# Moving the split weights and the gated tiles to other addresses of SBUF in a kernel of window attention and a SwiGLU gate

## The chip, the cores and the metric

The kernel runs on one core of a Trainium2 chip. The metric is the time of one execution on the device in microseconds; 855.66 us is the median of three runs of the kernel before.

## The reference

For 2048 tokens of width 512: a layer norm without scale or shift gives `xn`. Two branches read it. Branch A is attention with 32 heads of width 16, causal, each token seeing itself and the 255 before it, followed by an output projection. Branch B is a SwiGLU feed-forward with 1792 hidden columns. The output is `x + A * silu(B)`, all in float32.

```python
xn = layernorm(x)
q, k, v = split(xn @ wqkv)                    # 32 heads of 16
p = softmax(where(0 <= i - j < 256, q @ k.T / 4, -1e9))
s = (p @ v) @ wo
g = silu((silu(xn @ w_gate) * (xn @ w_up)) @ w_down)
return x + s * g
```

## The kernel before

**Splitting.** Every projection is computed from operands that are split into a high part (rounded to the type float32r) and a low part (what the rounding lost, also float32r). A product takes three matmuls: high by high, high by low and low by high; low by low is dropped (`PAIRS`). So each weight block exists as two tiles, `wh` and `wl`, the normed activations as `xh` and `xl` (together `xn`), the gated hidden values as one tile `hh` with both parts, and the attention output before `wo` as `oh`, which uses the same buffers as `hh`. Weights are split on the chip: a DMA brings a raw block `wr`, ScalarE rounds it into `wh` (line 474), GpSimd subtracts to get `wl` (line 459).

**Tiling.** The tokens are taken in four chunks of 512. The dense work is a list of 120 units, written out in `ORDER`: A (a pair of head groups' q and k), V (values), G (one block of 128 gate and up columns), D (a quarter of the hidden columns through the down projection, one half of the output columns) and W (`wo`). Unit number n of this list uses two pairs of weight buffers, numbers 2n and 2n+1 modulo 6. So a unit whose number leaves rest 0 after division by 3 has the buffers 0 and 1, rest 1 has 2 and 3, rest 2 has 4 and 5. The numbers are n = 2 for G0.0, 3 for G0.1, 113 for G3.13, 114 to 117 for D3.2.0, D3.2.1, D3.3.0 and D3.3.1, 118 and 119 for W3.0 and W3.1.

**Halves of TensorE.** Each contraction of 128 is done as two of 64: rows 0 to 63 of the array work on one item of a unit, rows 64 to 127 on another (line 491 for all dense matmuls, shown as `64*128`). The two halves run side by side, each with its own order, and meet only in the visits that multiply probabilities with values (`pv`, line 1204). Within a half every matmul needs its own weight load, and the load for the next matmul runs while the present one streams.

**Who is stationary and who moves.** In A and G the weights `wh`, `wl` are loaded into the array and 512 columns of `xh` or `xl` stream through. In V, D and W it is the other way round: 128 columns of activations (`xh`, `xl`; `hh`; `oh`) are loaded and 256 columns of weights stream. In the last chunk's W the activations stand in the buffers of `xn`. Attention scores (lines 1013 and 1167) load columns of q or k and stream up to 384 columns of k or q.

**The order of the work** is fixed when the program is built: a planner with estimated costs emits the instructions of all engines in one order, and only semaphores act at run time. The planner knows nothing of addresses.

**Addresses.** One tile pool (`pers`) holds everything in SBUF. A tile gets its place when its tag first appears in the program, one tag behind the other, each rounded up to 32 bytes; a tag that comes again reuses the place. The tiles that matter here and the rest of their byte address in a partition after division by 256, as the program before is laid out:

| tiles | address | modulo 256 |
|---|---|---|
| `q`, `k` | 19,200 to 49,920 | 0 |
| `xh`, `xl` (four tiles of 8192 bytes) | 67,840 to 100,608 | 0 |
| `gp` (the down projection's sums) | 100,608 | 0 |
| `p` (probabilities) | 109,376 | 64 |
| 12 tiles of 2048 bytes that are handed out for passing values | 136,704 on; 183,936 on | 0; 128 |
| `wr`, two tiles | 146,944; 159,296 | 0; 64 |
| `wh`, `wl` number 0 and 1 | 151,040 to 159,232 | 0 |
| `wh`, `wl` number 2 and 3 | 163,392 to 171,584 | 64 |
| `wh`, `wl` number 4 and 5 | 175,680 to 183,872 | 64 |
| `hh` buffer 7 | 171,584 | 64 |
| `hh` buffers 0 to 6 (also `oh`) | 198,272 to 228,736 | 128 |

Slices that one matmul reads start at multiples of 512 bytes inside these tiles, so the rests of the table are those of the operands.

Of the kernel before, what the change touches and what calls it, by code (L numbers as in the profile page):

```python
# [9 lines left out]
F32 = mybir.dt.float32  # L10
F32R = mybir.dt.float32r
# [6 lines left out]
P = 128  # L18
# [9 lines left out]
TC = 512  # L28
# [9 lines left out]
NHID = 8  # L38
# [27 lines left out]
def tile_window_attention_swiglu_gate(  # L66
# [12 lines left out]
    pers = ctx.enter_context(tc.tile_pool(name="pers", bufs=1))  # L79
# [122 lines left out]
    ks = [pers.tile([P, 2, HALO + TC], F32R, name=f"k{i}") for i in range(3)]  # L202
    vt = pers.tile([P, VT, VROW], F32, name="v")
    xn = [[pers.tile([P, KC, TC], F32R, name=f"x{'hl'[s]}{i}") for s in range(2)] for i in range(2)]
    gp = pers.tile([P, 4, D], F32, name="gp")

    def constants():
# [1246 lines left out]
    while True:  # L1454
        now[0] = max(front[0], min(clock))
        while marks and marks[-1][0] <= work[0] / PACE - LEAD:
            _, fn, a = marks.pop()
# [12 lines left out]
        if not any(extra):  # L1470
            s = work[0] / PACE - LEAD
# [67 lines left out]
```

## Time and profile before

| | us |
|---|---|
| median of three runs | 855.66 (853.76 to 855.67) |
| the profiled execution | 856.13 |
| its span, first to last instruction | 854.3 |
| TensorE matmul busy in the span | 847.2 (99%), 11,950 matmuls |
| weight loads | 786.4 (92%) |
| VectorE, ScalarE, GpSimd busy | 485.3, 496.5, 602.1 |
| the 16 DMA engines, mean busy share | 58.8% by the main queue |

In the profile, PE is TensorE, PEld its weight loads, DVE VectorE, ACT ScalarE, POOL GpSimd. A matmul's duration in it is its passage through the array, with its end modelled; matmuls of a half follow each other sooner than that duration. How fast a half works is read from the starts: the distance from the start of one matmul to the start of the next in the same half. The timeline gives starts to 0.01 us, so a run of ten or more matmuls gives that distance to about 1 ns.

### The profile page before, as it was taken

The page shows a single profiled execution, that of the slowest core. Times are in us where ns is not written, and L with a number is a line of the kernel's source. Part 1 is how long each engine was busy: PE and PEld are TensorE (multiplying, and loading weights), DVE is VectorE, ACT ScalarE, POOL GpSimd, SP SyncE. Part 2 cuts the span into 40 slices and gives each one's busy share as a digit, 9 for nine tenths or more (in the row PEclk, how much of TensorE's full clock was granted, in tenths as well). Part 3 has the DMA queues.
Part 4 walks back from the last instruction along what each step waited for, and adds up shares of the span by engine and source line. Part 5 has one row for each costly group of instructions (what it writes and reads, how often), then busy time and mean ns, then how long its engine had stood idle before and what let it go on. Part 6 is the DMA issues. An engine that isn't in the chain of part 4 may idle for free.

```text
span 854.3 us, 29720 instructions
## 1 busy us (share of the span) xinstructions
PE 847.2 (99%) x11950; PEld 786.4 (92%) x11950; DVE 485.3 (57%) x1628; ACT 496.5 (58%) x1055; POOL 602.1 (70%) x637
## 2 busy tenths in 40 slices
PE   9999999999999999999999999999999999999998
PEld 8899988989999999999999999989999989998998
DVE  4265465655566666555566765566665656554333
ACT  4345566555675566545677566565566766556532
POOL 7556566667686876655779784665667897868866
PEclk9999999999999999999999999999999999999999
DMA  4765554477677955355577886355656767724351
GB/s 152 212 190 166 159 151 136 120 191 182 160 186 207 282 148 129 102 134 154 149 198 197 215 211 196 112 142 154 170 122 165 197 191 205 193 84 147 114 157 57
DMA packets 67661, 139.59 MB, mean 163 GB/s; under 512 B 12722, under 2 KB 21426, under 8 KB 67524
## 3 DMA queue, kind: packets, MB, share of 16 engines
q1 hardware_dynamic: 67220, 137.17, 58.8%
q8 instruction: 94, 1.54, 0.8%
q10 hardware_dynamic: 304, 0.52, 0.2%
q14 instruction: 43, 0.35, 0.1%
HBM read 107.74 MB, written 29.62 MB: 161 GB/s over the span
## 4 chain that ended last, share of the span: by engine, by line
PE 96%; DMA 2%; POOL 1%; issue 1%; ACT 0%; DVE 0%; SPq 0%; POOLq 0%; DVEq 0%; ACTq 0%
PE u L491 19%; PE d L491 19%; PE g L491 17%; PE a L491 11%; PE pv L1204 8%; PE vp L491 5%; PE c L1167 5%; PE s L491 5%; PE b L1013 5%; DMA wr<-wdn 1%; DMA xt<-x 1%; PE xp L513 0%; POOL wl L459 0%; POOL rs L273 0%; POOL p L1141 0%
## 5 line engine op out<-in xcount | busy, mean ns | idle before, releaser
L459 POOL TENSOR_TENSOR wl<-wr,wh 128x512 fp32r<-128x512 f32 (+1 forms) x240 | 298.1, 1258 | 140.5 <-ACT wh L474 122.0
L1021 DVE CUSTOM_DVE_ANT_0 jk<-b,maskb 128x384 bf16<-128x384 f32 (+2 forms) x512 | 271.4, 530 | 124.2 <-PE b L1013 66.3
L1128 ACT ACTIVATE p<-c 128x384 f32<-128x384 f32 (+1 forms) x480 | 208.3, 496 | 128.7 <-PE c L1167 116.2
L491 PE MATMUL d<-wh,hh 64*128 64x256 f32 x1792 | 252.4, 279 | 0.0
L491 PEld LDWEIGHTS d<-wh,hh 64*128 64x128 f32 x1792 | 217.4, 185 | 0.4
L491 PE MATMUL d<-wl,hh 64*128 64x256 f32 x896 | 195.9, 279 | 0.0
L474 ACT ACTIVATE wh<-wr 128x512 fp32r<-128x512 f32 (+1 forms) x239 | 142.1, 619 | 62.5 <-PE u L491 15.4
L491 PE MATMUL g<-xh,wl 64*128 64x512 f32 x448 | 173.3, 396 | 0.6 <-issue 0.6
L491 PE MATMUL g<-xl,wh 64*128 64x512 f32 x448 | 173.4, 395 | 0.0
L491 PE MATMUL u<-xh,wl 64*128 64x512 f32 x448 | 173.1, 396 | 0.0
L491 PE MATMUL g<-xh,wh 64*128 64x512 f32 x448 | 172.9, 394 | 0.0
L491 PE MATMUL u<-xl,wh 64*128 64x512 f32 x448 | 172.7, 396 | 0.0
L491 PE MATMUL u<-xh,wh 64*128 64x512 f32 x448 | 171.6, 395 | 0.0
L491 PEld LDWEIGHTS d<-wl,hh 64*128 64x128 f32 x896 | 141.3, 185 | 0.8 <-issue 0.4
L1141 POOL TENSOR_SCALAR_AFFINE_SELECT p<-p 128x512 f32<-128x512 f32 x128 | 81.0, 636 | 73.6 <-ACT p L1128 71.7
L1013 PE MATMUL b<-k,q 48*128 48x384 f32 (+2 forms) x512 | 112.6, 331 | 0.0
L1167 PE MATMUL c<-q,k 49*128 49x384 f32 (+1 forms) x704 | 103.8, 294 | 0.0
L491 PE MATMUL a<-xl,wh 64*128 64x512 f32 (+1 forms) x264 | 93.1, 389 | 0.0
L491 PE MATMUL a<-xh,wl 64*128 64x512 f32 (+1 forms) x264 | 92.7, 389 | 0.1
L491 PE MATMUL a<-xh,wh 64*128 64x512 f32 (+1 forms) x264 | 92.6, 390 | 0.0
L491 PEld LDWEIGHTS u<-xl,wh 64*128 64x128 f32 x448 | 82.5, 185 | 3.8 <-issue 1.0
L491 PEld LDWEIGHTS u<-xh,wh 64*128 64x128 f32 x448 | 82.2, 185 | 3.4 <-DVE ho L488 0.4
(104 smaller groups left out, 2040.3 us busy)
## 6 DMA issues: line engine op xcount, KB each, us to landing
wr<-wgu SPq DMA_DIRECT2D x56, 512.0 KB
k<-qkd SPq DMA_DIRECT2D x48, 192.0 KB
wr<-wqk SPq DMA_DIRECT2D x16, 512.0 KB
qkd<-qkh SPq DMA_DIRECT2D x32, 256.0 KB
qkd<-qkl SPq DMA_DIRECT2D x32, 256.0 KB
q<-qkd SPq DMA_DIRECT2D x64, 128.0 KB
wr<-wdn SPq DMA_DIRECT2D x16, 512.0 KB
od<-ev SPq DMA_DIRECT2D x32, 256.0 KB
```

The costliest lines, as they stand in the source:

```text
L459: nc.gpsimd.tensor_tensor(lo, raw[j][:, n], f32(hi), op=ALU.subtract)
L474: do("S", t, 0.13 + 0.00078 * m, lambda: nc.scalar.activation(hi, raw[j][:, n], AF.Copy), after_high, sl)
L491: return nc.tensor.matmul(pb, a, b, start=first, stop=last, skip_group_check=True)
L1013: nc.tensor.matmul(pb[:, :w], qs[u % 3][r : r + 48, p, qb * P : (qb + 1) * P], ks[u % 3][r : r + 48, p, lo : lo + w], start=True, stop=True,)
L1021: nc.vector.tensor_tensor_reduce(junk[:, :n], pb[:, :n], maskb[:, 3 * P - n :], 1.0, -3.0e38, ALU.add, ALU.max, m[:, col : col + 1],)
L1128: nc.scalar.activation(t[:, h, :], pc[:, a:b], AF.Exp, scale=DH ** -0.5)
L1141: nc.gpsimd.affine_select(s, s, [[0, 4], [1, P]], ALU.is_ge, 0.0, base=0, channel_multiplier=-1)
L1167: nc.tensor.matmul(pc[:, at0 : at0 + w], ks[u % 3][r : r + 49, p, k0 : k0 + P], qs[u % 3][r : r + 49, p, qb * P : qb * P + w], start=(i == ...
L1204: nc.tensor.matmul(pbs[r][0][32 * j : 32 * j + 32, q0:q1], vt[half(r), (4 * c + kb) % VT, VW * (4 * g + j) : VW * (4 * g + j) + 32], t[hal ...
```

## The change

Right behind the four tiles of `xn` the program names the tags of the twelve split weight tiles, then a tile of 64 bytes that nothing uses, then the eight tags of the gated buffers. Nothing is computed with these tiles here; the names only fix where the tags lie. All later tiles, `gp`, `p`, the passing tiles and `wr` among them, move accordingly. No instruction is added, removed or moved.

```diff
     xn = [[pers.tile([P, KC, TC], F32R, name=f"x{'hl'[s]}{i}") for s in range(2)] for i in range(2)]
+    for n in range(6):
+        for s in "hl":
+            pers.tile([P, 512], F32R, name=f"w{s}_{n}", tag=f"w{s}{n}", bufs=1)
+    pers.tile([P, 16], F32, name="gap")
+    for n in range(NHID):
+        pers.tile([P, 2, TC], F32R, name=f"hr_{n}", tag=f"hr{n}", bufs=1)
     gp = pers.tile([P, 4, D], F32, name="gp")
```

## The prediction

> **What bounds the kernel now.** I read the page first, then the chain of work that ended last, then the groups of instructions by shape, and last the timeline of TensorE row by row, since the change acts on addresses alone and no summed view tells one buffer from another.
>
> ```profile
> span 854.3 us, 29720 instructions
> PE 847.2 (99%) x11950; PEld 786.4 (92%) x11950; DVE 485.3 (57%) x1628; ACT 496.5 (58%) x1055; POOL 602.1 (70%) x637
> PEclk9999999999999999999999999999999999999999
> PE 96%; DMA 2%; POOL 1%; issue 1%; ACT 0%; DVE 0%; SPq 0%; POOLq 0%; DVEq 0%; ACTq 0%
> ```
>
> TensorE is busy throughout at the full clock, and 96% of the chain is its own work. Whatever changes the rhythm of the matmuls shows in the time nearly one to one; 4% of the chain is something else and would not shrink. The two halves of the array run side by side, so the time follows the sum of the distances from start to start within one half.
>
> ```profile
> L491 PE MATMUL d<-wh,hh 64*128 64x256 f32 x1792 | 252.4, 279 | 0.0
> L491 PE MATMUL d<-wl,hh 64*128 64x256 f32 x896 | 195.9, 279 | 0.0
> L491 PE MATMUL g<-xl,wh 64*128 64x512 f32 x448 | 173.4, 395 | 0.0
> L491 PE MATMUL a<-xl,wh 64*128 64x512 f32 x248 | 90.9, 396 | 0.0
> L491 PE MATMUL vp<-wh,xh 64*128 64x256 f32 x256 | 59.2, 280 | 0.0
> L491 PE MATMUL s<-wh,oh 64*128 64x256 f32 x384 | 53.1, 280 | 0.0
> L459 POOL TENSOR_TENSOR wl<-wr,wh 128x512 fp32r<-128x512 f32 x224 | 286.7, 1295 | 127.9 <-ACT wh L474 110.5 <-DMA den<-od 6.9 <-PE c L1167 6.7
> ```
>
> There are 6 x 448 + 3 x 248 = 3432 matmuls of 512 columns in G and A, 1716 a half, and 2688 of D, 768 of V, 768 of W with 256 columns. Their durations (279, 395) hide the rhythm, so the starts decide. All the readings below are starts of one half.
>
> **What the rhythm depends on.** G0.0 (n = 2, weights at rest 64) and G0.1 (n = 3, weights at rest 0) ran side by side, one in each half; these are the first and last rows of either.
>
> ```profile
> 27.03 0.40 PE L491 MATMUL u<-xl,wh 64*128 64x512 f32 x1
> ...
> 27.28 0.39 PE L491 MATMUL g<-xh,wh 64*128 64x512 f32 x1
> ...
> 29.79 0.39 PE L491 MATMUL g<-xh,wl 64*128 64x512 f32 x1
> 29.82 0.39 PE L491 MATMUL u<-xl,wh 64*128 64x512 f32 x1
> ```
>
> `u` of G0.0 makes 12 steps in 2.79 us, 232.5 ns each; `g` of G0.1 makes 11 steps in 2.51 us, 228.2 ns each. The shape, the moving operand's rest (0) and the stretch of time are the same; what differs is where the weights lie. A second pair, `u` of G0.1 (10 steps) and, late and undisturbed by attention, `g` and `u` of G3.13 (n = 113, rest 64; 35 steps of one half):
>
> ```profile
> 33.20 0.39 PE L491 MATMUL u<-xl,wh 64*128 64x512 f32 x1
> ...
> 35.51 0.39 PE L491 MATMUL u<-xh,wl 64*128 64x512 f32 x1
> ...
> 809.83 0.39 PE L491 MATMUL g<-xh,wh 64*128 64x512 f32 x1
> ...
> 818.00 0.39 PE L491 MATMUL u<-xh,wl 64*128 64x512 f32 x1
> ```
>
> That is 2.31 us / 10 = 231.0 ns with weights at 0, and 8.17 us / 35 = 233.4 ns with weights at 64. Sorting all steps of 512 columns by the rest of the weights loaded meanwhile, stalls left out, gives 231.5 ns (1,357 steps) and 233.4 ns (1,734 steps), of which these rows are a part. The neighbour half's addresses make no difference in that sorting.
>
> For 256 columns I write (rest of the moving weights, rest of the loaded activations). D3.2.0 is (0, 128) and D3.2.1 is (64, 128); one row of low weights to the same row of the next block is three steps in either half.
>
> ```profile
> 822.15 0.39 PE L491 MATMUL d<-wl,hh 64*128 64x256 f32 x2
> ...
> 824.64 0.37 PE L491 MATMUL d<-wl,hh 64*128 64x256 f32 x2
> ...
> 825.71 0.33 PE L491 MATMUL d<-wl,hh 64*128 64x256 f32 x2
> ...
> 827.75 0.39 PE L491 MATMUL d<-wl,hh 64*128 64x256 f32 x2
> 828.57 0.28 PE L491 MATMUL d<-wl,hh 64*128 64x256 f32 x1
> ...
> 831.39 0.28 PE L491 MATMUL d<-wl,hh 64*128 64x256 f32 x1
> ```
>
> D3.2.0: 2.49 us / 21 = 118.6 ns. D3.2.1: 2.04 us / 18 = 113.3 ns. D3.3.0 in one half, mostly (64, 128) again: 2.82 us / 24 = 117.5 ns. So one placing shows two rhythms, and the better of them only where the rests differ by 64. Over the whole trace (0, 128) averages 118.7 ns (971 steps) and (64, 128) 117.0 (1,472). The last W is (64, 0) with 45 steps, V3.1 (n = 90) is (0, 0) with 14:
>
> ```profile
> 842.43 0.39 PE L491 MATMUL s<-wh,xl 64*128 64x256 f32 x2
> ...
> 847.73 0.39 PE L491 MATMUL s<-wh,xl 64*128 64x256 f32 x2
> ...
> 657.84 0.28 PE L491 MATMUL vp<-wh,xh 64*128 64x256 f32 x1
> ...
> 659.51 0.28 PE L491 MATMUL vp<-wh,xl 64*128 64x256 f32 x1
> ```
>
> (64, 0) takes 5.30 us / 45 = 117.8 ns and (0, 0) takes 1.67 us / 14 = 119.3 ns.
>
> **The change part by part.** *Where things land.* `xn` ends at 100,608, a multiple of 256. Twelve tiles of 2048 bytes end at 125,184, so every `wh` and `wl` has rest 0. 64 bytes later the eight gated buffers of 4096 bytes start at 125,248, rest 64, and end at 158,016. `gp` goes from 0 to 64, `p` from 64 to 128, the passing tiles from 0 and 128 to 64 and 192, `wr` from 0 and 64 to 64 and 128. The instructions, their order, the semaphores and the DMAs' sizes and queues stay.
>
> *G and A.* 1,837 of the 512-column steps, 918 a half, now have weights at 64 loaded under them and get weights at 0. A gain of 233.4 - 231.5 = 1.9 ns each over the whole trace; the quoted stretches bound it by 232.5 - 231.0 = 1.5 and 233.4 - 228.2 = 5.2. 918 steps at 1.5, 1.8 and 5.2 ns make 1.4, 1.65 and 4.8 us; I take -1.65, near the average, since it has all chunks in it.
>
> *D and the first six W.* All become (0, 64), the difference that (64, 128) has now. 496 steps a half come from (0, 128), 830 from (64, 128). If the difference decides, the first gain 118.7 - 117.0 = 1.7 ns and the others nothing: -0.85 us. (0, 64) does occur, where D loads from buffer 7 with weights at 0: 156 scattered steps, 118.0 ns on average, but each between two or three slower (0, 128) ones. At 118.0 the sum is -496 x 0.7 + 830 x 1.0 = +0.5 us. I take -0.6, most of the way to the first, because buffer 7's steps stand in slower company. Upper gain: 5.3 ns (118.6 - 113.3) for 496 steps, -2.6 us.
>
> *V and the last W.* They go from (64, 0) to (0, 0): 484 steps a half at +1.5 ns, +0.7 us by the two stretches.
>
> *Attention scores.* They stream k or q at rest 0, and 149 steps a half of 384 columns load weights from 64 meanwhile, later from 0. At three quarters of 1.8 ns that is -0.2 us; it may be nothing. `pv` streams `p`, whose rest shifts by 64, against value columns that start at every multiple of 4 bytes, so its 2,816 matmuls meet all differences before and after: nothing.
>
> *The other engines.* Their operands keep shape and type. GpSimd's subtraction has 127.9 us of idle time in front of its 224 pieces, and by its operands' rests its pieces average 1291 to 1307 ns; 13 ns on all is 2.9 us of an engine that is busy for 70%. What covers it is that idle time; were it gone, the 2.9 us would lie on the path. DMAs move the same rows of 2048 bytes.
>
> Sum: -1.65 - 0.6 + 0.7 - 0.2 = -1.75 us of TensorE's own time, of which the 4% of the chain that isn't TensorE takes nothing worth naming. On the profiled execution 856.13 - 1.75 = 854.4; that execution was 0.5 above the median of the runs, so on the median **853.9 us**, 0.2% less. With each term at its ends (1.4 to 4.8 off, 0.5 on to 2.6 off, 0.7 on, 0 to 0.3 off) the sum lies between -0.2 and -7.0.
>
> **The rivals.** *The better rhythm everywhere.* 228.2 and 113.3 ns show that the good placings can run faster than their averages. If, with all units alike, the halves settle there, the sum is -4.8 - 2.6 + 0.7 - 0.3 = -7.0: 848.7 us. Against it: half of the present good steps do not, even when the other half has a good placing too. Halfway is 851.
>
> *Nothing.* The addresses could be innocent, the difference coming from which unit stands where in the order. Then the time stays at 855.7. Against it speaks the first pair of rows, two units in the same 2.5 us. The Trainium skill would have it so: its page "SBUF — State Buffer", under "Who interferes with whom", gives TensorE two independent read ports, one for the moving operand and one for weight loads, and says that it never waits on anyone. By that rule 228.2 beside 232.5 ns ought not to occur in this trace, and the trace bears it out less than the placement.
>
> *Slower: the place of the moving weights counts, not the difference.* Every moving weight tile goes to rest 0, where 118.6 and 119.3 were read, while 113.3, 117.5 and 117.8 all have it at 64. Then 830 steps of D and W lose 118.6 - 117.0 = 1.6 ns on average (+1.3 us), up to 5.3 ns (+4.4 us), V loses its 0.7, and G gains at least its 1.4. That is +0.6 to +3.7: 856.3 to 859.4 us. It turns the sign from (1.4 - 0.7) / 830 = 0.8 ns per step of D. For it: 118.0 at (0, 64). Against it: the same 156 steps are still quicker than (0, 128) with the same moving place.
>
> **How the numbers follow.** The measurement can tell about 0.3% (2.6 us) from no change. The forecast, a gain of 0.7 to 3.0 us, has a chance of 0.52; the better rhythm 0.2; nothing 0.16; slower 0.1; 0.02 for anything else. Faster by over 0.3%, that is below 853.1, are the better rhythm and a third of the forecast's cases: 0.36. Slower by over 0.3% is the upper half of the last rival, with a little of the scatter: 0.07. The rest, 0.57, lies within. The range leaves out the far end of the better rhythm and of the slower case: 850.0 to 857.0; the forecast's own is 852.7 to 855.0.
>
> **What would show it.** In the changed kernel's timeline, G3.13 should step at 231 to 232 ns instead of 233.4, D3.2.0 below 118 instead of 118.6, and the last W at 119 instead of 117.8, which can be read without any comparison of totals. If D3.2.1 goes from 113.3 to 118.6 the slower rival is right; if G3.13 steps at 228 the better rhythm is. If G3.13 stays at 233.4, the addresses don't matter and the prediction is wrong at its root; if the steps move as said and the time does not, the share of TensorE in the chain was over-read.

## The result and the profile after

The median went from 855.04 us (four runs, 853.76 to 855.67) to 850.16 us (four runs, 849.08 to 850.75): a ratio of 0.9943 with a 95% interval of 0.9926 to 0.9961. In a later comparison on one chip it was 0.9941 (0.9929 to 0.9954). The kernel became 4.9 us faster; 853.9 had been forecast. 850.16 lies at the lower end of the range, between the forecast and the rival "better rhythm everywhere".

The page of the profiled execution (850.45 us) says where, with the same lines as before:

```profile
span 848.7 us, 29720 instructions
PE 842.0 (99%) x11950; PEld 782.0 (92%) x11950; DVE 484.6 (57%) x1628; ACT 496.4 (58%) x1055; POOL 602.8 (71%) x637
PEclk9999999999999999999999999999999999999999
PE 95%; DMA 2%; POOL 1%; issue 1%; DVE 0%; SPq 0%; ACT 0%; DVEq 0%; POOLq 0%
```

TensorE's busy time falls by 5.2 us and the span by 5.6; the other engines and the clock stay. GpSimd's subtraction, by shape, went from 1295 to 1299 ns:

```profile
L465 POOL TENSOR_TENSOR wl<-wr,wh 128x512 fp32r<-128x512 f32 x224 | 287.6, 1299 | 125.3 <-ACT wh L480 119.2 <-PE c L1173 3.9 <-PE b L1019 1.2
```

The stretches that the prediction named, in the timeline of TensorE (start, duration, engine, line, operation, operands, shape, count). Line 497 is the former line 491. First and last row of G3.13, of two stretches of D3.2 and D3.3, and of the last W, each pair from one half:

```profile
804.22 0.39 PE L497 MATMUL g<-xh,wh 64*128 64x512 f32 x1
...
812.18 0.39 PE L497 MATMUL u<-xh,wl 64*128 64x512 f32 x1
813.58 0.28 PE L497 MATMUL d<-wl,hh 64*128 64x256 f32 x1
...
816.06 0.28 PE L497 MATMUL d<-wl,hh 64*128 64x256 f32 x1
816.30 0.39 PE L497 MATMUL d<-wl,hh 64*128 64x256 f32 x2
...
831.85 0.28 PE L497 MATMUL d<-wl,hh 64*128 64x256 f32 x1
836.79 0.28 PE L497 MATMUL s<-wh,xh 64*128 64x256 f32 x1
...
842.18 0.28 PE L497 MATMUL s<-wh,xl 64*128 64x256 f32 x1
```

G3.13: 7.96 us in 35 steps, 227.4 ns, where it was 233.4. D: 2.48 us / 21 = 118.1 ns and 15.55 us / 132 = 117.8. The last W: 5.39 us / 45 = 119.8 ns, where it was 117.8. The W of the first three chunks have the same placing (0, 64) as D, and yet one half steps through W2.1 at 1.70 us / 15 = 113.3 ns:

```profile
724.97 0.27 PE L497 MATMUL s<-wh,oh 64*128 64x256 f32 x1
...
726.67 0.27 PE L497 MATMUL s<-wh,oh 64*128 64x256 f32 x1
```

So one placing still has two rhythms after the change, as it had before.

For the whole trace I put every distance from start to start in a half to the unit whose matmul began it, and took the mean of the two halves. Waits are in it. How the distances at the edges of the `pv` visits are shared out moves the levels of the columns, hardly the differences between rows. In us, with the experiments that are told below:

| | G | A | D | W | V | scores | pv | rest | sum |
|---|---|---|---|---|---|---|---|---|---|
| before | 332.3 | 96.3 | 166.9 | 48.3 | 48.0 | 92.2 | 49.7 | 10.1 | 843.8 |
| after | 329.0 | 96.2 | 164.9 | 47.5 | 48.4 | 92.7 | 49.6 | 10.0 | 838.3 |
| weights alone | 329.1 | 96.8 | 168.0 | 48.1 | 48.5 | 92.2 | 49.3 | 11.4 | 843.2 |
| gated alone | 331.6 | 96.3 | 166.7 | 47.5 | 47.9 | 92.3 | 49.3 | 10.1 | 841.7 |
| no gap | 328.6 | 95.7 | 168.7 | 48.8 | 48.3 | 92.2 | 49.7 | 10.0 | 842.0 |
| gap 192 | 328.8 | 95.7 | 166.9 | 47.9 | 48.4 | 92.1 | 49.3 | 10.0 | 839.0 |
| gap 224 | 329.0 | 95.7 | 166.2 | 48.1 | 48.4 | 92.1 | 49.3 | 10.0 | 838.9 |

G gained 3.3 us, D 2.0, W 0.8; V and the scores lost 0.9 together. The execution before that was profiled lies 1.1 us above its median and the one with the weights alone 2.4 above its own, so a sum is good to one or two us; single columns agree better, which the G column of the five kernels with all weights at rest 0 shows (328.6 to 329.1).

### The profile page after: what moved, and what is told of

Read it like the earlier page. It is cut to its first block, busy times and chain, and to the rows that moved or that the text cites. A ratio compares the mean times of both kernels' runs of the same rounds, so it can differ in the third digit from the quotient of the medians.

```text
span 848.7 us, 29720 instructions
## 1 busy us (share of the span) xinstructions
PE 842.0 (99%) x11950; PEld 782.0 (92%) x11950; DVE 484.6 (57%) x1628; ACT 496.4 (58%) x1055; POOL 602.8 (71%) x637
## 4 chain that ended last, share of the span: by engine, by line
PE 95%; DMA 2%; POOL 1%; issue 1%; DVE 0%; SPq 0%; ACT 0%; DVEq 0%; POOLq 0%
PE u L497 19%; PE d L497 19%; PE g L497 18%; PE a L497 11%; PE pv L1210 8%; PE c L1173 6%; PE vp L497 5%; PE b L1019 5%; PE s L497 5%; DMA wr<-wdn 1%; DMA wr<-wqk 1%; PE xp L519 0%; POOL wl L465 0%; DVE jk L1027 0%; SPq L105 0%
## 5 line engine op out<-in xcount | busy, mean ns | idle before, releaser
L497 PE MATMUL d<-wl,hh 64*128 64x256 f32 x896 | 193.6, 278 | 0.0
L497 PEld LDWEIGHTS d<-wl,hh 64*128 64x128 f32 x896 | 138.4, 186 | 0.6 <-issue 0.4
L1173 PE MATMUL c<-q,k 49*128 49x384 f32 (+1 forms) x704 | 105.6, 295 | 0.0
```

Source lines behind the costliest of these rows:

```text
L497: return nc.tensor.matmul(pb, a, b, start=first, stop=last, skip_group_check=True)
L1173: nc.tensor.matmul(pc[:, at0 : at0 + w], ks[u % 3][r : r + 49, p, k0 : k0 + P], qs[u % 3][r : r + 49, p, qb * P : qb * P + w], start=(i == ...
```

## The experiments

**One part alone.** If the gain is made of separate terms, each half of the change should bring its own. The first kernel names only the weights early, so that all of them lie at rest 0 and D is (0, 128) everywhere, except with buffer 7:

```diff
+    for n in range(6):
+        for s in "hl":
+            pers.tile([P, 512], F32R, name=f"w{s}_{n}", tag=f"w{s}{n}", bufs=1)
```

> Only the split weights are named early, so all of them lie at rest 0; gated buffers stay at 128 (one at 64) and every other tile at its rest of before. By the difference: G gains what it gained in the full change (g and u 3.3 us of a half's time), but D turns into (0,128) throughout: its 830 good steps lose 1.7 ns (+1.4 us) by the averages, V loses 0.4 us. Sum about -1.5 us, ratio 0.998. If the weights' place alone makes the gain, the ratio is that of the full change, 0.994. If D at (0,128) loses as much as the quickest rows suggest (118.6 against 113.3), D costs +4.4 us and the time is 0.5 us above before.

The second names only the gated buffers and leaves the weights at 0 and 64:

```diff
+    pers.tile([P, 16], F32, name="gap")
+    for n in range(NHID):
+        pers.tile([P, 2, TC], F32R, name=f"hr_{n}", tag=f"hr{n}", bufs=1)
+    pers.tile([P, 48], F32, name="rest")
```

> Only the gated buffers are named early, behind 64 bytes, and 192 bytes after them give all other tiles their rests of before; so D has (0,64) in a third of its units and (64,64) in two thirds, G and V stay as before. By the difference: the (0,128) steps gain 2.5 ns (-1.2 us), the (64,128) steps turn into difference 0 and lose 1.6 ns (+1.3 us), so about 0, ratio 0.999 to 1.002. If the place of the gated buffers alone makes D quicker, D gains 2 us as in the full change, ratio 0.9975.

Against 854.70 us before in the same comparison, both came out level: 854.06 us, 0.9997 (0.9986 to 1.0007), where 0.998 had been expected and lies just outside, and 854.36 us, 0.9997 (0.9988 to 1.0006), inside what was expected. The timeline of the weights alone, G3.13 and D3.2 in one half:

```profile
812.92 0.39 PE L494 MATMUL u<-xh,wh 64*128 64x512 f32 x1
...
818.13 0.39 PE L494 MATMUL u<-xh,wl 64*128 64x512 f32 x1
819.57 0.28 PE L494 MATMUL d<-wl,hh 64*128 64x256 f32 x1
...
826.77 0.28 PE L494 MATMUL d<-wl,hh 64*128 64x256 f32 x1
```

G has its whole gain (5.21 us / 23 = 226.5 ns, column G as after), but D at (0, 128) runs at 7.20 / 60 = 120.0 ns in this stretch, and D loses 1.1 us against before. By the columns G, D, W and V, 1.8 us of gain are left; the median shows 0.6. Part of what hides the rest is the granted clock. Five of the twelve executions had a mean granted clock of 0.996 to 0.998 and took 854.87 to 857.31 us; the other seven, at 0.999 or 1.000, took 852.68 to 854.26 with a median of 852.94, and the 21 such executions of before have 854.68. The profiled execution is one of the five; the view by stretches gives it a clock of 0.57 (the third number from the end) between 11 and 15 us:

```profile
11.00:15.00 4.00, 4.00 (x22) 3.02 (x23) 2.26 (x6) 2.14 (x8) 3.35 (x5) 0.57 0.03 11
```

So the weights alone are probably worth near the 1.5 us that was expected, though the whole comparison doesn't tell it from nothing. Whether it is chance that 5 of 12 executions lost clock here and 2 of 23 before is open. And the gated buffers alone:

```profile
810.81 0.39 PE L495 MATMUL u<-xh,wh 64*128 64x512 f32 x1
...
816.17 0.40 PE L495 MATMUL u<-xh,wl 64*128 64x512 f32 x1
816.53 0.27 PE L495 MATMUL d<-wl,hh 64*128 64x256 f32 x1
...
819.93 0.27 PE L495 MATMUL d<-wl,hh 64*128 64x256 f32 x1
821.97 0.27 PE L495 MATMUL d<-wl,hh 64*128 64x256 f32 x1
...
831.67 0.28 PE L495 MATMUL d<-wl,hh 64*128 64x256 f32 x1
```

G3.13 stays at 5.36 us / 23 = 233.0 ns. D3.2.0 with (0, 64) runs at 3.40 / 30 = 113.3 ns, and the D behind it, now (64, 64), at 9.70 / 81 = 119.8. So neither part carries the whole gain: the gated buffers can stand at one distance from all weights only once the weights stand together, and the weights' gain in G is partly paid back in D while the buffers stand at 128.

**The place or the difference.** The full change, with 64 bytes more put ahead of all these tiles: weights at 64, gated buffers at 128, activations at 64. All differences stay, all places are others.

```diff
+    pers.tile([P, 16], F32, name="lead")
```

> The full change with 64 bytes more ahead of everything, so every tile's rest moves by 64 and every difference stays. By the difference: the time of the full change, ratio 0.994 against before, within 0.001. If a place counts for itself (rest 0 for what streams in G, 64 for what is loaded in D), the gain is gone or turned: 0.998 to 1.002.

849.87 us, 0.9945 (0.9933 to 0.9957), the same as the change.

```profile
806.42 0.39 PE L498 MATMUL u<-xh,wh 64*128 64x512 f32 x1
...
811.63 0.39 PE L498 MATMUL u<-xh,wl 64*128 64x512 f32 x1
815.75 0.39 PE L498 MATMUL d<-wl,hh 64*128 64x256 f32 x2
...
830.94 0.39 PE L498 MATMUL d<-wl,hh 64*128 64x256 f32 x2
```

G3.13 at (64, 64): 226.5 ns over 23 steps. D at (64, 128): 15.19 us / 129 = 117.8 ns, as with (0, 64). No share of the place can be told; the slower rival falls.

**The other tiles.** The change also moves `gp`, `p`, `wr` and the passing tiles. Here the full change has 192 bytes more behind the gated buffers, so that these tiles come back to their former rests; the change itself ran again beside it.

```diff
+    pers.tile([P, 48], F32, name="rest")
```

> The full change with 192 bytes more behind the gated buffers, so weights and gated buffers lie as in the change and all other tiles (sums, probabilities, passing tiles, raw weights) have their rests of before. If only the operands of the dense matmuls count: the time of the full change, ratio 0.994 to 0.9955. If the probabilities' or passing tiles' place has a share in the 4.9 us: that share is lost, ratio above 0.996.

> The full change once more, for a comparison on the same chip: 0.994, all theories.

849.43 us, 0.9943 (0.9929 to 0.9956), against 849.74 us, 0.9941 (0.9929 to 0.9954). The other tiles have no share that can be told.

**The 64 bytes.** The whole change without the tile `gap`: weights and gated buffers both at rest 0.

```diff
     for n in range(6):
         for s in "hl":
             pers.tile([P, 512], F32R, name=f"w{s}_{n}", tag=f"w{s}{n}", bufs=1)
-    pers.tile([P, 16], F32, name="gap")
```

> The weights named early and the gated buffers right behind them, without the 64 bytes between: weights and gated buffers both at rest 0, everything else as before. G, A, V and the last W keep what the change gave them; D and the first six W, 1326 steps a half, go from (0, 64) to (0, 0). If the address difference decides, they lose between 118.25 - 116.1 = 2.15 ns (the averages of the changed kernel) and 120.0 - 116.1 = 3.9 ns (undisturbed series): 2.9 to 5.2 us over the changed kernel's 849.7, so 852.6 to 854.9, ratio 0.998 to 1.000 to the kernel before. If all units having the same difference were what counts, whatever that difference is, it stays at 849.7, ratio 0.994.

853.39 us, 0.999 (0.9981 to 0.9999), inside what was expected if the difference decides. D runs at 16.20 us / 135 = 120.0 ns:

```profile
819.74 0.40 PE L496 MATMUL d<-wl,hh 64*128 64x256 f32 x2
...
835.94 0.28 PE L496 MATMUL d<-wl,hh 64*128 64x256 f32 x1
```

D and W together cost 217.5 us instead of 212.4; the sum grows by 3.7, since G, A and the scores came out 1.4 lower. By the ratios the 64 bytes are worth 3 to 4 us, most of the gain, and that all units have one common difference is worth little if it is a bad one.

**The pace by itself.** Three kernels measure the rhythm away from the kernel: they bring `x` to SBUF, round it into one tile to stream and one to load from, run series of matmuls with a new weight load each, and copy `x` to the output; the reference is not computed. The pace of a series is the distance from its start to the next series' start, divided by its matmuls in one half: 24 of 512 columns, and 48 of 256 columns in the first kernel, 32 in the others. The change-over from the series before is in it.

> This kernel computes nothing of the reference: it copies x to the output and, beside that, runs series of 24 (512 columns) or 48 (256 columns) float32r matmuls in either half of TensorE, with the start of the moving operand and of the loaded operand set to chosen rests modulo 256, nothing else using SBUF by then. If the difference of the two rests decides (my theory): 512 columns at (0,0) and (64,64) step alike, at about 227.5 ns as in the changed kernel's undisturbed stretches, (0,64) at 233; 256 columns at (0,64) and (64,128) alike, 113 to 118 ns, (0,0) and (64,64) alike at 119.5, (0,128) at 118.7. If the place of the moving operand decides (the slower rival): (64,64) and (0,0) differ by more than 1 ns, (64,128) is quicker than (0,64). If only neighbours and stalls make the differences (nothing): all of one width within 1 ns. If the other half matters, the half at (0,0) beside one at (0,64) steps at more than 229 ns, and the series with one half alone are quicker than those with both.

```profile
31.54 5.63 PE L83 MATMUL ga<-m,l 64*128 64x512 f32 x48
36.99 5.77 PE L83 MATMUL gb<-m,l 64*128 64x512 f32 x48
42.58 5.78 PE L83 MATMUL gc<-m,l 64*128 64x512 f32 x48
48.18 5.79 PE L83 MATMUL gd<-m,l 64*128 64x512 f32 x48
...
137.99 0.27 PE L83 MATMUL di<-m,l 64*128 64x256 f32 x1
...
143.43 0.27 PE L83 MATMUL dj<-m,l 64*128 64x256 f32 x1
...
148.87 0.28 PE L83 MATMUL dk<-m,l 64*128 64x256 f32 x1
...
154.63 0.28 PE L83 MATMUL pa<-m,l 64*128 64x256 f32 x1
```

`ga` is (0, 0), `gb` (0, 32), `gc` (0, 64): 5.45, 5.59 and 5.60 us by 24 make 227.1, 232.9 and 233.3 ns. `di` is (64, 128), `dj` (64, 0), `dk` (64, 64): 5.44, 5.44 and 5.76 us by 48 make 113.3, 113.3 and 120.0 ns. By the same reading, all differences in steps of 32 bytes (loaded less streamed):

| difference | 0 | 32 | 64 | 96 | 128 | 160 | 192 | 224 |
|---|---|---|---|---|---|---|---|---|
| 512 columns, ns | 227.1 | 232.9 | 233.3 | 233.8 | 233.3 | 233.8 | 229.2 | 233.3 |
| 256 columns, ns | 119.8 | 118.1 | 117.9 | 117.5 | 118.3 | 119.8 | 117.7 | 117.9 |

With no kernel around it, (64, 64) again goes with (0, 0): 120.0 and 119.8 ns for 256 columns; for 512 columns 228.3 and 227.1 over the whole series, which is just over the 1 ns that the expectation allowed, but 226.7 for both in the second half of the series. Two halves with different placings keep their own pace side by side (227.2 and 233.3 ns). But (64, 128) at 113.3 and (0, 64) at 117.9 have the same difference, and that was the other sign of the rival that the place decides. The two series stood behind different neighbours, so the next kernels enter each difference from several series. The first of them used one half of the array alone.

> Computes nothing of the reference: it copies x and times series of float32r matmuls in one half of TensorE, the other half idle. Moving operand at rest 0, loaded operand at rests 0 to 240 in steps of 16; 256 columns entered three ways (after a series at 120 ns, after a 512-column series at 227 ns, after 128-column matmuls), 512 columns entered two ways (after a series at 233 ns and after one of 256 columns). My theory after the first series: the rhythm is a matter of this difference alone, in steps of 6.7 ns (113.3, 120.0; 226.7, 233.3), and some differences have two rhythms, of which the entry picks one; then (0,64) shows 113.3 after one entry and 117.8 after another, (0,0) at 512 columns 226.7 after both. Rival: the difference alone decides, with no memory; then the entries agree within 0.5 ns at every difference, and the two rhythms of the same placing in the kernels come from the rows and columns of the real operands.

The series `wb` is 512 columns at (0, 0), `dse` 32 matmuls of 256 columns at (0, 64). The last row is of the view by stretches: busy time of TensorE, of its loads, of the other engines, and then the granted clock, 1.00.

```profile
22.05 10.44 PE L126 MATMUL wb<-m,l 64*128 64x512 f32 x24
32.29 10.44 PE L126 MATMUL wc<-m,l 64*128 64x512 f32 x24
...
165.41 7.03 PE L126 MATMUL dse<-m,l 64*128 64x256 f32 x32
172.24 3.61 PE L126 MATMUL zf<-m,l 64*128 64x512 f32 x8
```

```profile
400.00:500.00 100.00, 100.00 (x431) 96.01 (x430) 0.00 (x0) 0.00 (x0) 0.00 (x0) 1.00 0.00 0
```

10.24 us / 24 = 426.7 ns and 6.83 us / 32 = 213.4 ns, for every difference. The run settles nothing about the entry: the array worked at half its pace for all 917 us. The clock of 1.00 is no evidence against that: the page of this run has no row PEclk, and the view gives 1.00 wherever the trace holds no record of the clock. It does so too for the first kernel (here TensorE alone: busy time, clock, DMA), whose matmuls of 512 columns step at 427 ns between 14.1 and 18.0 us:

```profile
10.00:15.00 5.00, 3.57 (x14) 1.00 1.05 406
```

The first clock record of that trace begins at 18.3 us, where its steps go from 427 to 227 ns. The trace of one half alone has no such record. The next kernel has the same series in both halves.

> The series of the run before, now in both halves at once, since with one half alone the array worked at half the pace throughout (a row of 512 columns at 426.7 ns whatever the addresses) and told nothing. The kernel copies x to its output and computes nothing else of the reference. With the pace at full speed each address difference from 0 to 240 in steps of 16 bytes is entered in three ways (256 columns) or two (512 columns). If the address difference alone fixes the rhythm, the series of one difference agree to 0.5 ns whatever stood before them: 226.7 or 233.3 ns for 512 columns, 113.3, 117.8 or 120.0 for 256. If the rhythm is kept from what stood before as well, the same difference shows two of these values, by entry. If 64 bytes are the grain, the three differences between two multiples of 64 go with one of them; if 32, pairs do.

In its timeline `gsb` and `gfb` are both 24 steps at (0, 16), `dsm` and `dfm` both 32 steps at (0, 192), `dso` 32 steps at (0, 224); the rows between are the series that stand ahead of them.

```profile
220.57 3.81 PE L126 MATMUL dsm<-m,l 64*128 64x256 f32 x64
224.20 2.02 PE L126 MATMUL zf<-m,l 64*128 64x512 f32 x16
226.04 3.95 PE L126 MATMUL dfm<-m,l 64*128 64x256 f32 x64
229.81 0.69 PE L126 MATMUL zt<-m,l 64*128 64x128 f32 x10
...
250.58 3.92 PE L126 MATMUL dso<-m,l 64*128 64x256 f32 x64
254.32 2.02 PE L126 MATMUL zf<-m,l 64*128 64x512 f32 x16
...
295.45 5.79 PE L126 MATMUL gsb<-m,l 64*128 64x512 f32 x48
301.06 1.60 PE L126 MATMUL zf<-m,l 64*128 64x256 f32 x24
302.47 5.64 PE L126 MATMUL gfb<-m,l 64*128 64x512 f32 x48
307.93 2.05 PE L126 MATMUL zs<-m,l 64*128 64x512 f32 x16
```

(0, 192): 3.63 us / 32 = 113.4 ns behind 256 columns at (0, 0), 3.77 / 32 = 117.8 behind 512 columns at (0, 0), and 117.8 behind 128 columns. (0, 64) is the other way about: 117.8 ns behind the first two, 113.3 behind 128 columns once it has settled. (0, 16): 5.61 us / 24 = 233.8 behind 512 columns at (0, 64), 5.46 / 24 = 227.5 behind 256 columns at (64, 0); the second steps at 227 ns from its fourth step to its end, the first never does. So the rhythm belongs to the difference and to what ran before, and lasts. (0, 64) with 113.3 and 117.8 also answers the first kernel: the place is not needed to explain its two values. Other differences have one rhythm whatever stood before: (0, 64) with 512 columns 233.4, (0, 224) with 256 columns 3.74 / 32 = 116.9, later 116.6. A difference of 16 bytes can change it, so neither 64 nor 32 bytes is the grain.

**Another gap.** Two versions of the change that these paces suggest, with all other tiles at the rests that they had before the change. The edit against the change:

```diff
-    pers.tile([P, 16], F32, name="gap")
+    pers.tile([P, 48], F32, name="gap")
...
+    pers.tile([P, 16], F32, name="rest")
```

> The change with 192 bytes between weights and gated buffers instead of 64, all else at its old rest: D and the first six W at (0, 192). The separate measurement has 113.3 ns there after slow series of 256 columns and 117.8 after others, the mirror image of (0, 64), which had 113.3 only after series of 128 columns. If the kernel's D units settle as in the first, they step at 113.3 undisturbed, the steps gain up to 2.8 ns on 116.1: 846.0 us, ratio 0.990. If as in the second, 117.8 undisturbed as with 64 and the time stays at 849.7, up to 852 if the disturbed stretches lose their better steps as well.

and the same with 56 and 8 columns in place of 48 and 16:

> The change with 224 bytes between weights and gated buffers, all else at its old rest: D and the first six W at (0, 224). There the separate measurement has 116.7 ns whatever stood before. If that holds in the kernel, the undisturbed D units step at 116.7 instead of 117.8, and over all 1326 steps a half the average comes near 116.7 to 117 instead of 116.1: 849.7 + 0.8 to 1.2 us, about 850.5 to 850.9, ratio 0.995 to 0.996. If only multiples of 64 count, it goes with 192.

```profile
813.29 0.30 PE L498 MATMUL d<-wl,hh 64*128 64x256 f32 x2
...
827.77 0.28 PE L498 MATMUL d<-wl,hh 64*128 64x256 f32 x1
```

```profile
817.46 0.35 PE L498 MATMUL d<-wl,hh 64*128 64x256 f32 x2
...
832.52 0.34 PE L498 MATMUL d<-wl,hh 64*128 64x256 f32 x2
```

The first rows are of 192 bytes, the second of 224. 192 bytes: 14.48 us / 123 = 117.7 ns, the slower of the two rhythms that this difference showed. 851.35 us, 0.9959 (0.9946 to 0.9971). 224 bytes: 15.06 us / 129 = 116.7 ns, as in the separate series, 1.1 ns better than the change in this stretch; but over the whole trace D costs 166.2 us instead of 164.9, since the change has stretches of 15 steps and more at 113 to 115 and this version has none. 850.12 us, 0.9943 (0.9930 to 0.9957), a little better than the 850.5 to 850.9 expected: D and W together cost 1.9 us more than in the change, but A, the scores and `pv` came out 1.4 lower. Neither beats the change; 224 is level with it.

## Why the prediction was right, and where it was off

*The bound.* Right: TensorE's own time fell by 5.2 us of the 5.6 of the span, and the other engines' work stayed as it was.

*The difference decides.* Right, and shown: moving everything by 64 bytes left 0.9945, taking the 64 bytes between weights and buffers away left 0.999. It isn't all that decides: for some differences the pace depends on what ran before as well. "Slower" and "nothing" both fall. The Trainium skill's page "SBUF — State Buffer", section "Who interferes with whom", gives TensorE two independent read ports and no waiting; these runs differ from it, with 227.1 and 233.3 ns for two addresses of the loaded operand, and the measurement decides. What in the chip makes the difference count was not measured. Nor do the runs tell the operand that is being loaded from the one already in use: in every unit and series both lie at the same rest.

*G and A.* The sign was right, the size half: -3.4 us (G 3.3, A 0.1) against -1.65. The step that failed is "918 steps a half gain 1.8 ns", which left the steps that already had weights at 0 where they were. They improved too: (0, 0) averages 230.6 ns over 3,087 steps after, against 231.5 over 1,357 before. Together 2.0 ns on 1,716 steps, 3.4 us. The prediction saw that good placings could run at 228 and didn't find what kept them from it. The traces show part of it, when the steps are counted from the last time that the half did other work (attention, or a unit that is neither G nor A). After the change the first three steps of 512 columns average 232.1 ns (1,545 of 2,500 steps of G and A), the fourth to seventh 228.8 (682), all later ones 227.4 (273). Before, with the weights at 64, the same three classes have 233.4, 233.3 and 233.1. So the good placing needs a few steps to settle, and in the mixed kernel most steps are among the first. This is read from the order of the steps; no run changes that order.

Two readings of the prediction are off without harm. Of the 12 steps given to `u` of G0.0 the last two load weights of G0.1, at rest 0. The stretch called D3.3.0 is the last block of D3.2.1 in the other half, with the same placing (64, 128): one unit stepped at 113.3 ns in one half and 117.5 in the other.

*D and the first six W.* Mis-sized: -0.6 forecast, -2.8 measured with the last W in it, whose loss was put elsewhere. The step that failed is the average of 117.0 to 118.0 ns that (64, 128) and (0, 64) had before, taken for what (0, 64) would have. After the change (0, 64) averages 116.1 ns over 2,781 steps, with stretches at 113.3 among those at 117.8. Here the long undisturbed stretches are not the quick ones: counted in the same way, from the last work that was neither D nor W, the fourth to fifteenth steps average 115.0 ns (1,410), those from the sixteenth on 117.6 (374). And the same placing held 113.3 for 30 steps with the gated buffers alone. Both values had been read before; how often which would come could not be read from a trace in which the differences alternate.

*V and the last W.* +0.7 forecast. V lost 0.4, and the last W's steps cost 119.8 - 117.8 = 2.0 ns each in the quoted stretch, which makes 0.1 us for its 45 steps. Somewhat less, and the sign right.

*Scores, `pv`, the other engines.* Forecast -0.2 and nothing; the sums moved by +0.5 for the scores and -0.1 for `pv`. The prediction looked at the weights loaded under the scores and not at the gated tiles, whose (0, 128) at 180.9 ns became (0, 64) at 181.6 for 197 steps; the whole row is within what one profile can tell.

*The sum.* -1.75 forecast, -4.9 measured by the medians. The named stretches came out as follows: G3.13 at 227.4 is the mark of "better rhythm everywhere" and not of the forecast's 231 to 232; D3.2.0 at 117.8 to 118.1 is only just the forecast's "below 118"; the last W at 119.8 is as forecast. So the better rhythm came in the undisturbed stretches of 512 columns and for 256 columns in part; over all steps 512 columns came down to 230.6 ns, not to 227. The forecast's own range of 852.7 to 855.0 missed the time. The range with the rivals in it held it, close to its end: 850.16 against 850.0. That is partly luck: the four executions run from 849.08 to 850.75, and the repeated comparison gave 849.74, against a before of 854.45.

## What to carry to other kernels

Where every matmul has its own weight load, the byte address of the operand that is loaded, less that of the operand that streams, taken modulo 256, changes the pace by up to 3% (512 columns) and 6% (256 columns) in the separate series; it can be set by naming tags in another order and costs no instruction. Measure the pace of the pairs of tiles in both halves of the array, with what precedes them, and lay out all tiles that meet each other at once: here each half of the layout alone came out level within the noise, and both together gave 0.6%. When a trace shows two rhythms for one placing, an average over a mixed program is a poor forecast of a uniform one.

## What had not been expected of the hardware

Settled, 512 columns step at 226.7 ns at the difference 0 and 233.3 at 64, and 256 columns at 120.0 and at 113.3 or 117.8. These are not the only values: with the difference 192, 512 columns settle at 228.9. A series can keep the rhythm that it was entered with to its end, 24 to 32 steps later, so two series with the same addresses can differ by 6.3 ns a step (227.5 and 233.8).

One half of the array alone, from the first matmul on, ran 512 columns at 426.7 ns for 917 us, and the addresses made no difference then. In the first separate kernel one half alone ran at 228.3 ns right after both halves had worked (5.48 us for 24 steps). The Trainium skill's page "TensorE: Matmul & The Clock Gate", section "Back-to-back issue gap", gives the gap in ns as the columns divided by 1.2 while the array is cold, that is, not yet released by sustained work; the estimate from it is 426.7 for 512, and this run agrees. The same page's "Part 1: The HAM clock gate" has the array released after about 3.4 us of sustained work; here a steady stream of one half did not release it in 917 us. Why was not measured. A clock of 1.00 in the profile doesn't exclude this state: look for the row PEclk, and at the starts.
